# The next-to-last chunk's routing runs as one block ahead of the last units' masks, and its scatters run beside each other

## The chip, the cores and the metric

The kernel runs on one core of a Trainium2 chip. Times are microseconds on the device for one execution; of several executions the median is given. In the rows of the trace the engines are PE (TensorE, matrix products), PEld (its weight loads), DVE (VectorE), ACT (ScalarE), POOL (GpSimd) and SP (SyncE, which here only issues transfers; SPq and POOLq are the parts of SP and GpSimd that issue). L785 is line 785 of the kernel before.

## What is computed

The reference has two stages. The first is a linear attention with a complex decay, for 4 batches, 8 heads, 768 time steps and head size 48. The second is a mixture of experts on its output: 3072 tokens of 384 values, 8 experts, each token sent to at most one.

```python
for t in range(S):                       # first stage
    ar, ai = (a_re_n[:, :, t, :, None], a_im_n[:, :, t, :, None])
    new_re = ar * S_re - ai * S_im
    new_im = ar * S_im + ai * S_re
    kv = np.einsum('bhd,bhe->bhde', k[:, :, t], v[:, :, t])
    S_re, S_im = (new_re + kv, new_im)
    y[:, :, t] = np.einsum('bhd,bhde->bhe', q[:, :, t], S_re)
...
do_compute = x @ w_skip > 0              # second stage, x is y by token
e_idx = np.argmax(xc @ w_gate, axis=1)   # xc: the tokens with do_compute
...
h = np.maximum(xc[mask] @ w1[e], 0.0)    # mask: the tokens of expert e
y[mask] = gate_w[mask, None] * (h @ w2[e])
out[do_compute] = xc + y                 # the others pass unchanged
```

## The kernel before

**Attention.** The 768 steps are cut into 6 chunks of 128 steps (`c` from 0 to 5), and each chunk into 4 units, one for each batch (`b`). A unit forms its scores `pa` on TensorE (`unit_at`), masks them into `at` on VectorE (L657, two halves), and combines them with the state of the chunks before. For the last chunks (`late`) that is done with two products on VectorE, `RX` (L667 with the state, L668 with a copy of the state whose halves are swapped, `T2`, made by two transfers, L641), and their sum, `st` (L679). Then come the output `py` (L703 from `at`, L706 from `st`), its copy `yT`, and the product `px` (L713), which turns the rows into token order and at once gives the 9 routing numbers per token. The rows go to `xa`, and from there to the output (L727).

**Routing.** For chunks 0 to 4, `route` works on all four batches together. From the routing numbers `lg` it makes, on VectorE, the sum over heads `lgs` (L805), the best expert, and `oh`, which marks it; TensorE counts the tokens ahead of each one that go to the same expert (L827 to L830); VectorE then makes the row `sl` (L852) in a table `xs` in device memory, which holds 240 rows for each expert. `place` scatters each batch's 128 tokens to these rows with an indirect transfer that GpSimd issues (L785). The scheduler knows that all of them write `xs`, so each waits for the one before, except those of chunk 5, for which `place` declares that they don't touch the same rows. Chunk 5's routing is done for each unit by itself (`route1`, `rest`).

**Experts.** Expert 0's input is put together on TensorE without waiting for all scatters: chunk 5's tokens are picked by products with a one-hot matrix `ohx` (L1053), and those of chunks 0 to 4 are read from `xs` into the tile `early` (L744) and transposed into the same sums (L1050). Chunk 5's own scatters wait for that read. Experts 1 to 7 get their rows by `xg` (L1017) from `xs`. Weights come by SP into four buffers (L998), and ScalarE and VectorE split each one in two (L1009, L1010). The expert products are L1085 and L1117 to L1119.

**What sets the order.** The kernel is written as generators (`units`, `router`, `weights` and others), and `Order` decides, by a priority and by estimated times, which one writes its next instructions. A scheduler then lays the instructions out for each engine; `tc.issue_after(x)` keeps an instruction behind `x`. Each engine works through its own list in order, and so does SP. The tile tagged `T2` has one buffer: the next unit's copy can only be made when this unit's L668 has read it.

Of the kernel before, what the change touches and what calls it, by code (L numbers as in the profile page):

```python
# [24 lines left out]
NCH = S // C  # L25
# [14 lines left out]
BIG = float(1 << 20)  # L40


P_UNIT, P_ROUTE, P_CONSUME, P_REST, P_GATE, P_WEIGHTS = 0.5, 0.7, 1, 1, 2, 3

SHARE = 1.8
CREDIT = 600.0
# [66 lines left out]
class Kern:  # L113
# [530 lines left out]
    def unit(self, c, b):  # L644
# [8 lines left out]
        pa = self.pa.pop((c, b))  # L653
        for hh in range(2):

            with self.tc.issue_after(self.cins):
                self.at_ins = V.tensor_tensor(at[:, hh * 4:hh * 4 + 4], pa[hh],  # L657
                                              self.mask.rearrange("p (o t) -> p o t", o=1).to_broadcast([128, 4, C]),
                                              ALU.mult).ins
            yield o.wait(vt(512), 0 if hh == 0 or c == 0 else self.rx_t)  # L660
        late = self.last(c)
        Fb = self.F[:, :, b * H:(b + 1) * H].unsqueeze(3) if c > 0 else None
        if c > 0:
            T = self.T[b]
            X = self.un.tile([96, 2, H, D], F32, name=f"RX_{nm}", tag="RX", bufs=1)
            if late:
                V.tensor_tensor(X[:, 0], T, Fb[:, 0].to_broadcast([96, H, D]), ALU.mult)  # L667
                V.tensor_tensor(X[:, 1], self.T2.pop(b), Fb[:, 1].to_broadcast([96, H, D]), ALU.mult)  # L668
            else:
                with self.tc.issue_after(self.cins):  # L670
                    V.tensor_tensor(X, T.unsqueeze(1).to_broadcast([96, 2, H, D]), Fb.to_broadcast([96, 2, H, D]), ALU.mult)
# [42 lines left out]
        self.px_ins = pe.ins  # L714
        xa = self.xa[:, b]
        if c == NCH - 1:
            V.tensor_reduce(self.lg[:, b], px[:, :, 2 * D:].rearrange("p h e -> p e h"), AX.X, ALU.add)
        else:
            A.copy(self.lg[:, b], px[:, :, 2 * D:])
        if c == NCH - 1:  # L720
# [16 lines left out]
    def early(self):  # L737

        m = self.rt.tile([128, B * XW], F32, name="early", tag="xa", bufs=2)
        o = self.un.tile([128, B, CAP], F32R, name="ohx", tag="qkT")  # L740
        nx = 2 * DM
        self.xe = m[0:TP, 0:nx].rearrange("p (t d) -> p t d", d=DM)
        self.ohx = [o[:, b] for b in range(B)]
        self.early_ins = self.nc.sync.dma_start(self.xe, self.xs[0:CAP, 0:DM].rearrange("(t p) d -> p t d", p=TP)).ins  # L744

    def units(self, g):
        self.nat(2 * g, 0)
        self.nat(2 * g, 1)
        self.unit_at(2 * g, 0)
        for cc in range(2):  # L750
            c = 2 * g + cc
            while self.routes_done < c - 1:
                yield 0, 200
            if c > 0:
                yield from self.make_F(c - 1)
            if c < NCH - 1:
                self.lg = self.rt.tile([128, B, H // 2, E + 1], F32, name=f"lg_{c}", tag="lg", bufs=2)
            else:
                self.lg = self.rt.tile([128, B, E + 1], F32, name=f"lg_{c}", tag="lg5")
            self.xa = self.rt.tile([128, B, XW], F32, name=f"xa_{c}", tag="xa", bufs=2)  # L760
            if c == NCH - 1:
                self.parts = [self.un.tile([128, B, DM], F32R, name=f"xa{k}", tag="nat") for k in "hl"]
            self.nc.gpsimd.tensor_copy(self.xa[:, :, DM], self.tok[:, :, c])
            for b in range(B):

                while self.cpos < min((g + 1) * (HC + 1) + (cc * B + b) * PACE, NG * (HC + 1)):
                    yield 0, 100
                yield from self.unit(c, b)
                self.units_done += 1
            if c < NCH - 1:  # L770
                self.routes.append((self.lg_t, self.route(c, self.lg, self.xa)))

    def router(self):

# [9 lines left out]
    def place(self, c, b, sl, xa):  # L784
        x = self.nc.gpsimd.indirect_dma_start(out=self.xs, out_offset=bass.IndirectOffsetOnAxis(ap=sl, axis=0),  # L785
                                              in_=xa[:, b], in_offset=None, bounds_check=E * CAP - 1, oob_is_err=False).ins

        if c == NCH - 1:
            for y in self.scat:
                self.tc.declare_no_dep(x, y, reason="no two tokens have the same row")  # L790
            self.behind(x, [self.early_ins])
            self.scat.append(x)

    def route(self, c, lgp, xa):
# [27 lines left out]
        yield tiny, 130  # L822
        V.tensor_tensor(oh, self.iota8, b1(am), ALU.is_equal)
        yield sm, 130
        V.tensor_tensor(oh, oh, b1(act), ALU.mult)
        pr = self.ps_m.tile([128, B, E], F32, name=f"pr_{c}", tag="m")
        PE.matmul(pr, self.tri, oh, start=True, stop=False)  # L827
        PE.matmul(pr, self.ones, self.ohs.unsqueeze(1).to_broadcast([128, B, E]), start=False, stop=False)
# [20 lines left out]
        sl = self.rt.tile([128, B], I32, name=f"sl_{c}", tag="sl", bufs=4)  # L849
        V.tensor_tensor(rk, rk, base, ALU.add)  # L850
        yield tiny, 130
        V.tensor_tensor(sl, rk, ov, ALU.add)  # L852
        for b in range(B):
            self.place(c, b, sl[:, b:b + 1], xa)
        yield tiny, 0
# [9 lines left out]
    def route1(self, b):  # L865

        V, PE = self.nc.vector, self.nc.tensor
        c = NCH - 1
        T = lambda name, sh, dt=F32: self.rt.tile([128, B] + sh, dt, name=f"{name}_{c}", tag=name)
        iota = self.iota8[:, 0]  # L870
        sm, tiny = vt(8), vt(1)
        if b == 0:
            self.r5 = [T(k, []) for k in ("mx", "am", "act")] + [T("cand", [E]), T("oh", [E], BF16), T("dl", [E])]
            self.pr5 = self.ps_s.tile([128, B, E], F32, name="pr5", tag="ps")
        mx, am, act, cand, oh, dl = self.r5
        one = lambda t: t[:, b:b + 1]
        L, pr = self.lg[:, b, 0:E], self.pr5[:, b]
        V.tensor_reduce(one(mx), L, AX.X, ALU.max)
        yield sm, 70
        V.scalar_tensor_tensor(cand[:, b], L, one(mx), iota, ALU.is_equal, ALU.mult)  # L880
        yield sm, 70
        V.tensor_scalar(one(act), self.lg[:, b, E:], 0.0, None, ALU.is_gt)
        V.tensor_reduce(one(am), cand[:, b], AX.X, ALU.min)
        yield sm + tiny, 70
        V.scalar_tensor_tensor(oh[:, b], iota, one(am), one(act).to_broadcast([128, E]), ALU.is_equal, ALU.mult)
        PE.matmul(pr, self.tri, oh[:, b], start=True, stop=False)
        for k in range(b):
            PE.matmul(pr, self.ones, oh[:, k], start=False, stop=False)
        self.pr_ins[b] = PE.matmul(pr, self.ones, self.ohs, start=False, stop=True).ins
        pt = self.order.pe(200)  # L890
        hi, lo = [t[:, b] for t in self.parts]
        V.tensor_tensor(lo, self.xa[:, b, 0:DM], hi, ALU.subtract)
        yield self.order.wait(vt(DM), pt)
        if b == 0:
            self.early()

        val = T("val", [])[:, 0:1]
        V.scalar_tensor_tensor(val, oh[:, b, 0:1], -BIG, pr[:, 0:1], ALU.mult, ALU.add)
        yield tiny, 70
        V.tensor_scalar(self.ohx[b], self.iotac, BIG, val, ALU.subtract, ALU.is_equal)  # L900
        yield vt(CAP), 0
        if b >= B - 2:
            self.order.add(P_REST, self.rest(0 if b == B - 2 else b, b + 1))
# [436 lines left out]
```

## Time and profile before

| what | us |
|---|---|
| median of 3 runs | 531.55 |
| lowest and highest of them | 530.05, 532.46 |
| the profiled execution, its own time | 526.55 |
| its span in the trace | 524.8 |
| TensorE busy | 406.7 (77% of the span) |
| VectorE busy | 405.9 (77%) |
| ScalarE busy | 301.3 (57%) |
| GpSimd busy | 99.1 (19%) |

Shares of the whole span say little here, since the stages differ: in the first VectorE is the fullest engine, in the second (from about 380 us) TensorE. A wait between the two stages is in neither share. The granted clock is given as a part of TensorE's full speed.

### The profile page before, as it was taken

How to read it: one execution, taken by the hardware profiler on the slowest of the kernel's cores; microseconds unless marked ns; L12 is line 12 of the kernel's file. 1: busy time of each engine (PE TensorE's matmuls, PEld its weight loads, DVE VectorE, ACT ScalarE, POOL GpSimd, SP SyncE). 2: the span in 40 equal slices, each digit the busy share in tenths (PEclk: the TensorE clock that was granted, in tenths of full speed). 3: DMA queues.
4: the chain of work that ended last, by engine and by line, in shares of the span. 5: the costliest groups of instructions: out<-in, count | busy, mean ns of one | idle time of the engine just before them, and what ended most of it. 6: DMA issues, size and time to landing. Idle time of an engine off the chain costs nothing. (4 is left out here: it accounts for less than half of the span.)

```text
span 524.8 us, 9901 instructions
## 1 busy us (share of the span) xinstructions
PE 406.7 (77%) x3200; PEld 353.3 (67%) x3200; DVE 405.9 (77%) x1051; ACT 301.3 (57%) x685; POOL 99.1 (19%) x174
## 2 busy tenths in 40 slices
PE   0347534499899304999999999986399999999993
PEld 0125322379777202887888889976399999999993
DVE  3899988989999999989789747877079678666731
ACT  5778867655557754788868651333066547554620
POOL 4002011111122544000000321201311112111011
PEclk9966777579999656999999999999599999999998
DMA  5557876679989887777555358556268678666400
GB/s 95 114 109 176 187 177 140 140 180 218 226 194 228 209 201 188 192 169 169 135 141 134 81 137 276 151 141 214 71 185 275 217 248 253 180 212 229 118 22 25
DMA packets 165217, 88.63 MB, mean 169 GB/s; under 512 B 138939, under 2 KB 158860, under 8 KB 165159
## 3 DMA queue, kind: packets, MB, share of 16 engines
q1 hardware_dynamic: 158135, 72.09, 54.1%
q0 software_dynamic: 5936, 15.65, 10.6%
q8 instruction: 27, 0.44, 0.4%
q10 hardware_dynamic: 1088, 0.20, 0.2%
q14 instruction: 31, 0.25, 0.2%
HBM read 63.19 MB, written 26.58 MB: 171 GB/s over the span
## 5 line engine op out<-in xcount | busy, mean ns | idle before, releaser
L496 PE MATMUL sw<-ws,ident 128*128 128x384 f32 x84 | 44.9, 672 | 36.3 <-ACT ws L482 36.3
L413 DVE TENSOR_TENSOR X<-W,ain 128x192 f32<-128x192 f32 x192 | 67.8, 353 | 3.5 <-ACT ain L339 0.2
L1010 DVE TENSOR_TENSOR l<-r,h 128x768 fp32r<-128x768 f32 (+1 forms) x53 | 56.5, 1072 | 11.2 <-ACT h L1009 11.2
L1087 ACT ACTIVATE hh<-ph 128x240 fp32r<-128x240 f32 x64 | 23.8, 374 | 56.3 <-PE ph L1085 56.1
L496 PEld LDWEIGHTS sw<-ws,ident 128*128 128x128 f32 x84 | 19.4, 254 | 48.7 <-ACT ws L482 39.0
L1009 ACT CAST h<-r 128x768 fp32r<-128x768 f32 (+1 forms) x53 | 49.1, 934 | 4.9 <-DMA r<-in_moe_w_dram 4.6
L422 DVE TENSOR_TENSOR W<-X 128x96 f32<-128x96 f32 x192 | 48.8, 254 | 3.6
L1085 PE MATMUL ph<-xh,l 128*128 128x240 f32 x192 | 51.2, 274 | 0.0
L1085 PE MATMUL ph<-xh,h 128*128 128x240 f32 x192 | 49.6, 274 | 0.0
L1085 PE MATMUL ph<-xl,h 128*128 128x240 f32 x192 | 49.5, 276 | 0.0
L578 PE MATMUL tp<-ident,iw 128*96 128x128 f32 x128 | 22.8, 324 | 30.1 <-DVE iw L514 25.6
L585 ACT COPY qk<-tp 96x256 f32<-96x256 f32 x128 | 39.7, 369 | 7.8 <-PE tp L578 7.6
L1117 PE MATMUL po<-h,hh 128*120 128x384 f32 x128 | 43.2, 338 | 0.0
L1118 PE MATMUL po<-l,hh 128*120 128x384 f32 x128 | 42.9, 337 | 0.0
L657 DVE TENSOR_TENSOR at<-pa,mask 128x512 f32<-128x512 f32 x48 | 32.3, 684 | 11.1 <-PE pa L635 7.0
L1119 PE MATMUL po<-h,hl 128*120 128x384 f32 x128 | 40.9, 341 | 0.0
L785 POOL DMA_INDIRECT xs<-xa,sl x24 | 26.9, 1120 | 73.9 <-DVE sl L852 20.6
L703 PE MATMUL py<-at,vt 128*64 128x128 f32 x384 | 40.4, 282 | 0.0
L578 PEld LDWEIGHTS tp<-ident,iw 128*96 128x96 f32 x128 | 17.3, 151 | 34.1 <-issue 10.9
L635 PE MATMUL pa<-qk 96*128 96x128 f32 x256 | 35.9, 289 | 4.3 <-DVE at L657 4.0
L635 PEld LDWEIGHTS pa<-qk 96*128 96x128 f32 x256 | 32.0, 197 | 8.5 <-DVE at L657 5.3
L1088 DVE SCALAR_TENSOR_TENSOR hl<-ph,hh 128x240 fp32r<-128x240 f32 x64 | 25.7, 403 | 14.8 <-ACT hh L1087 14.7
(241 smaller groups left out, 1062.0 us busy)
## 6 DMA issues: line engine op xcount, KB each, us to landing
r<-in_moe_w_dram SPq DMA_DIRECT2D x24, 512.0 KB, 4.7
r<-in_moe_w_dram SPq DMA_DIRECT2D x32, 384.0 KB, 4.0
nat<-kq SPq DMA_DIRECT2D x8, 768.0 KB, 5.4
kq<-nw POOLq DMA_DIRECT2D x24, 192.0 KB, 3.7
kq<-iw POOLq DMA_DIRECT2D x24, 192.0 KB, 2.9
vt<-in_v_dram SPq DMA_DIRECT2D x24, 192.0 KB, 3.3
out_dram<-xa SPq DMA_DIRECT2D x24, 192.0 KB, 3.2
ain<-in_a_im_dram SPq DMA_DIRECT2D x90, 48.0 KB, 2.5
```

What stands on the lines that cost most here:

```text
L413: V.tensor_tensor(X, prev.unsqueeze(1).to_broadcast([128, 2, 2, D]), windows(ain[:, j]), ALU.mult)
L422: self.cins = V.tensor_tensor(W[:, j, ::-1], X[:, :, 0], X[:, :, 1], ALU.add).ins
L496: nc.tensor.matmul(sw, self.ident, ws[:, :, c], start=(c == 0), stop=(c == 1))
L578: nc.tensor.transpose(tp[:, jj], src[:, s * 4 + jj], self.ident)
L635: nc.tensor.matmul(pa[h // 4][:, h % 4], KT(h), QT(h), start=True, stop=True)
L703: PE.matmul(py[j * 64:j * 64 + 64, hp], vt_[:, 2 * hp + j], at[:, 2 * hp + j], start=True, stop=(c == 0))
L1009: nc.scalar.copy(hi[:, ks], raw)
L1010: nc.vector.tensor_tensor(lo[:, ks], raw, hi[:, ks], ALU.subtract)
L1085: pe = PE.matmul(ph, w[:, k, js], x[:, k], start=(n == 0), stop=(n == len(terms) - 1))
L1117: PE.matmul(po, hh[:, j, sl], w2h[:, j], start=(j == 0), stop=False)
L1118: PE.matmul(po, hh[:, j, sl], w2l[:, j], start=False, stop=False)
L1119: pe = PE.matmul(po, hl[:, j, sl], w2h[:, j], start=False, stop=(j == NF - 1))
```

## The change

Chunk 4's routing (`c == NCH - 2`) is no longer handed to the `router` but runs with a higher priority than the units (`P_SOON`), and the instructions of units 2 and 3 of chunk 5 on VectorE (masks and state products) are kept behind it (`pin`, `rins`). Its four scatters are declared not to touch the same rows, as chunk 5's were, and `early` waits for all four (`behind`). Unit 0 of chunk 5 copies its routing numbers with ScalarE, and VectorE sums them later, when the routing of chunk 4 is done.

```diff
-P_UNIT, P_ROUTE, P_CONSUME, P_REST, P_GATE, P_WEIGHTS = 0.5, 0.7, 1, 1, 2, 3
+P_SOON, P_UNIT, P_ROUTE, P_CONSUME, P_REST, P_GATE, P_WEIGHTS = 0.4, 0.5, 0.7, 1, 1, 2, 3
...
-            with self.tc.issue_after(self.cins):
+            pin = self.rins if c == NCH - 1 and b >= 2 else self.cins
+            with self.tc.issue_after(pin):
                 self.at_ins = V.tensor_tensor(at[:, hh * 4:hh * 4 + 4], pa[hh],
...
             if late:
-                V.tensor_tensor(X[:, 0], T, Fb[:, 0].to_broadcast([96, H, D]), ALU.mult)
-                V.tensor_tensor(X[:, 1], self.T2.pop(b), Fb[:, 1].to_broadcast([96, H, D]), ALU.mult)
+                with self.tc.issue_after(pin):
+                    V.tensor_tensor(X[:, 0], T, Fb[:, 0].to_broadcast([96, H, D]), ALU.mult)
+                    V.tensor_tensor(X[:, 1], self.T2.pop(b), Fb[:, 1].to_broadcast([96, H, D]), ALU.mult)
...
         if c == NCH - 1:
-            V.tensor_reduce(self.lg[:, b], px[:, :, 2 * D:].rearrange("p h e -> p e h"), AX.X, ALU.add)
+            lgp = px[:, :, 2 * D:]
+            if b == 0:
+                self.lg0 = self.rt.tile([128, H // 2, E + 1], F32, name=f"lg_{nm}", tag="lg0")
+                A.copy(self.lg0, lgp)
+            else:
+                V.tensor_reduce(self.lg[:, b], lgp.rearrange("p h e -> p e h"), AX.X, ALU.add)
...
         self.early_ins = self.nc.sync.dma_start(self.xe, self.xs[0:CAP, 0:DM].rearrange("(t p) d -> p t d", p=TP)).ins
+        self.behind(self.early_ins, self.scat)
...
-            if c < NCH - 1:
+            if c < NCH - 2:
                 self.routes.append((self.lg_t, self.route(c, self.lg, self.xa)))
+            elif c < NCH - 1:
+                self.order.add(P_SOON, self.soon(c, self.lg_t, self.route(c, self.lg, self.xa)))
+
+    def soon(self, c, t, r):
+        while self.routes_done < c:
+            yield 0, 100
+        yield self.order.wait(0, t)
+        yield from r
...
-        if c == NCH - 1:
+        if c >= NCH - 2:
             for y in self.scat:
                 self.tc.declare_no_dep(x, y, reason="no two tokens have the same row")
-            self.behind(x, [self.early_ins])
+            if c == NCH - 1:
+                self.behind(x, [self.early_ins])
             self.scat.append(x)
...
-        V.tensor_tensor(oh, oh, b1(act), ALU.mult)
+        ins = V.tensor_tensor(oh, oh, b1(act), ALU.mult).ins
+        if c == NCH - 2:
+            self.rins = ins
...
-        V.tensor_tensor(sl, rk, ov, ALU.add)
+        ins = V.tensor_tensor(sl, rk, ov, ALU.add).ins
+        if c == NCH - 2:
+            self.rins = ins
...
+        while self.routes_done < c:
+            yield 0, 100
         if b == 0:
+            V.tensor_reduce(self.lg[:, 0], self.lg0.rearrange("p h e -> p e h"), AX.X, ALU.add)
             self.r5 = [T(k, []) for k in ("mx", "am", "act")] + [T("cand", [E]), T("oh", [E], BF16), T("dl", [E])]
```

What this does to the engines' lists is seen at three places. Names end in the number of a buffer; `RX_5_2` is unit 2 of chunk 5, and `lgs_4` belongs to chunk 4.

VectorE before, from the first instruction of chunk 4's routing: its small instructions alternate with the masks and state products of units 2 and 3.

```order
L805 TENSOR_REDUCE lgs_4_4138<-lg_4_3811 128x36
L667 TENSOR_TENSOR RX_5_2_4254<-T_4_2_3974,F_4_4068 96x384
L810 TENSOR_REDUCE mx_4_4140<-lgs_4_4138 128x4
L821 TENSOR_SCALAR act_4_4142<-lgs_4_4138 128x4
L668 TENSOR_TENSOR RX_5_2_4254<-T2_5_2_4186,F_4_4068 96x384
L812 TENSOR_TENSOR cand_4_4147<-lgs_4_4138,mx_4_4140 128x32
L814 TENSOR_TENSOR dl_4_4148<-lgs_4_4138,mx_4_4140 128x32
L657 TENSOR_TENSOR at_5_2_4218<-pa_5_2_0_4176,mask_71 128x512
L817 TENSOR_TENSOR cand_4_4147<-cand_4_4147,iota8_94 128x32
L679 SCALAR_TENSOR_TENSOR st0_165<-RX_5_2_4254,sg_86 96x8x48
L834 TENSOR_REDUCE se_4_4143<-dl_4_4148 128x4
L819 TENSOR_REDUCE am_4_4141<-cand_4_4147 128x4
```

VectorE now, from the same instruction, and then the end of the routing:

```order
L822 TENSOR_REDUCE lgs_4_4139<-lg_4_3811 128x36
L827 TENSOR_REDUCE mx_4_4141<-lgs_4_4139 128x4
L838 TENSOR_SCALAR act_4_4143<-lgs_4_4139 128x4
L829 TENSOR_TENSOR cand_4_4148<-lgs_4_4139,mx_4_4141 128x32
L831 TENSOR_TENSOR dl_4_4149<-lgs_4_4139,mx_4_4141 128x32
L834 TENSOR_TENSOR cand_4_4148<-cand_4_4148,iota8_94 128x32
L836 TENSOR_REDUCE am_4_4142<-cand_4_4148 128x4
L853 TENSOR_REDUCE se_4_4144<-dl_4_4149 128x4
```

```order
L864 TENSOR_REDUCE rk_4_4147<-cand_4_4148 128x4
L866 TENSOR_SCALAR ov_4_4146<-rk_4_4147 128x4
L869 TENSOR_TENSOR rk_4_4147<-rk_4_4147,base_4_4145 128x4
L877 SCALAR_TENSOR_TENSOR todo_113<-ov_4_4146,act_4_4143 128x4
L871 TENSOR_TENSOR sl_4_4223<-rk_4_4147,ov_4_4146 128x4
L658 TENSOR_TENSOR at_5_2_4219<-pa_5_2_0_4177,mask_71 128x512
L658 TENSOR_TENSOR at_5_2_4219<-pa_5_2_1_4178,mask_71 128x512
L896 TENSOR_REDUCE lg_5_4083<-lg_5_0_4133 128x9
```

The 22 instructions of the routing, from `lgs` to `sl`, now stand in one piece; before, 18 instructions of units 0 to 3 stood among them. The two masks of unit 2 now come behind `sl`.

TensorE before, from the second half of unit 2's scores (`pa_5_2_1`): the counting matmuls `pr_4` came 12 rows later, within unit 3's scores.

```order
L635 MATMUL pa_5_2_1_4177<-qk_2_1_2168 128x128 x4
L635 MATMUL pa_5_3_0_4258<-qk_2_1_2168 128x128 x4
L713 MATMUL px_5_0_4128<-wg_100,yT_5_0_4126 128x105 x4
L703 MATMUL py_5_1_4190<-at_5_1_4137,vt1_164 64x128 x2
L706 MATMUL py_5_1_4190<-qk_2_1_2168,st1_166 64x128 x2
```

TensorE now:

```order
L635 MATMUL pa_5_2_1_4178<-qk_2_1_2168 128x128 x4
L846 LDWEIGHTS tri_75
L846 MATMUL pr_4_4160<-oh_4_4150,tri_75 128x32
L847 LDWEIGHTS ones_78
L847 MATMUL pr_4_4160<-ohs_111,ones_78 128x32
L849 LDWEIGHTS ones_78
L849 MATMUL pr_4_4160<-oh_4_4150,ones_78 128x24
L849 LDWEIGHTS ones_78
L849 MATMUL pr_4_4160<-oh_4_4150,ones_78 128x16
L849 LDWEIGHTS ones_78
L849 MATMUL pr_4_4160<-oh_4_4150,ones_78 128x8
L715 MATMUL px_5_0_4128<-wg_100,yT_5_0_4126 128x105 x4
```

The five counting matmuls moved ahead of unit 0's `px` and unit 1's `py`.

SP before, from the copies of the swapped state for unit 3 (`T2_5_3`) to `early`:

```order
L641 DMA T2_5_3_4268<-T_4_3_4039 48x384 x2
L727 DMA out_0_dram<-xa_5_4084 128x384
L632 DMA vt1_164<-in_v_dram 128x8x48
L727 DMA out_0_dram<-xa_5_4084 128x384 x2
L998 DMA r3_1_0_4562<-in_moe_w1_dram 128x1024
L998 DMA r3_1_1_4566<-in_moe_w1_dram 128x1024
L998 DMA r3_1_2_4570<-in_moe_w1_dram 128x1024
L998 DMA r8_1_0_4576<-in_moe_w2_dram 128x2x384
L727 DMA out_0_dram<-xa_5_4084 128x384
L744 DMA early_4339<-xs_117 120x2x384
```

SP now, from the first output write of chunk 5:

```order
L734 DMA out_0_dram<-xa_5_4084 128x384
L632 DMA vt1_164<-in_v_dram 128x8x48
L641 DMA T2_5_3_4274<-T_4_3_4039 48x384 x2
L751 DMA early_4307<-xs_117 120x2x384
L734 DMA out_0_dram<-xa_5_4084 128x384 x2
L1022 DMA r3_1_0_4564<-in_moe_w1_dram 128x1024
L1022 DMA r3_1_1_4568<-in_moe_w1_dram 128x1024
L1022 DMA r3_1_2_4572<-in_moe_w1_dram 128x1024
L1022 DMA r8_1_0_4578<-in_moe_w2_dram 128x2x384
```

The two copies of `T2_5_3` moved behind an output write and a load of `v`, and `early` moved from the end of this piece to directly behind these copies: it now stands ahead of two output writes and of the first four weight loads of expert 1 (`r3_1_0` to `r8_1_0`).

## Rows read from the trace of the kernel before

**Rows 1.** The page's slices of the whole span, 13.1 us each.

```profile
PE   0347534499899304999999999986399999999993
```

**Rows 2.** Chain that ended last, 353 to 384: start, us, what.

```profile
367.00 0.97 DMA xs<-xa,sl
370.09 2.42 DMA xs<-xa,sl
372.72 3.50 DMA early<-xs
```

**Rows 3.** Timeline of POOL: start, us, engine, line, operation, out<-in, idle before.

```profile
356.83 1.00 POOL L785 DMA_INDIRECT xs<-xa,sl  x1 [18.47 <-DVE xal L892]
359.92 0.97 POOL L785 DMA_INDIRECT xs<-xa,sl  x1 [2.08 <-ACT dl L916]
377.01 0.97 POOL L785 DMA_INDIRECT xs<-xa,sl  x1 [5.95 <-DMA early<-xs]
380.85 0.97 POOL L785 DMA_INDIRECT xs<-xa,sl  x1 [0.30 <-ACT xh L1056]
```

**Rows 4.** Timeline of VectorE (DVE), columns as in rows 3.

```profile
344.94 0.39 DVE L805 TENSOR_REDUCE lgs<-lg 128x36 f32<-128x144 f32 x1
351.01 0.55 DVE L668 TENSOR_TENSOR RX<-T,F 96x384 f32<-96x384 f32 x1 [0.73 <-DMA T<-T]
353.74 0.60 DVE L679 SCALAR_TENSOR_TENSOR st<-RX,sg 96x384 f32<-96x384 f32 x1
355.88 0.15 DVE L852 TENSOR_TENSOR sl<-rk,ov 128x4 int32<-128x4 f32 x1
361.63 0.17 DVE L922 TENSOR_SCALAR ov<-rk 128x3 f32<-128x3 f32 x1
361.83 0.16 DVE L926 TENSOR_TENSOR rk<-rk,base 128x3 f32<-128x3 f32 x1
```

**Rows 5.** Timeline of TensorE (PE), columns as in rows 3.

```profile
345.71 1.16 PE L635 MATMUL pa<-qk 96*128 96x128 f32 x8
358.48 0.39 PE L706 MATMUL py<-qk,st 96*64 96x128 f32 x4
363.62 0.17 PE L889 MATMUL pr<-ohs,ones 128*128 128x8 bf16 x1
376.27 2.92 PE L1050 MATMUL pt<-ident,early 120*128 120x120 f32 x12 [12.48 <-DMA early<-xs]
380.20 0.27 PE L1085 MATMUL ph<-xh,h 128*128 128x240 f32 x1
```

**Rows 6.** Busy us by stretch: PE, PEld, DVE, ACT, POOL, clock, DMA, GB/s.

```profile
345.71:363.79 18.08, 16.08 (x191) 14.77 (x189) 14.80 (x81) 6.04 (x15) 1.98 (x2) 1.00 0.54 151
364.00:376.00 12.00, 0.00 (x0) 0.00 (x0) 0.99 (x9) 0.00 (x0) 1.94 (x2) 0.60 0.47 162
376.00:380.20 4.20, 3.93 (x18) 3.93 (x19) 0.12 (x1) 0.36 (x1) 2.58 (x3) 0.51 0.12 44
380.20:400.00 19.80, 19.80 (x151) 19.63 (x150) 16.77 (x38) 12.60 (x23) 2.70 (x5) 1.00 0.73 216
165.00:205.00 40.00, 13.57 (x85) 8.92 (x84) 38.35 (x130) 23.35 (x52) 21.12 (x28) 0.63 0.81 193
```

**Rows 7.** Timeline of SP's DMA issues, columns as in rows 3.

```profile
347.37 1.15 SPq L641 DMA_DIRECT2D T<-T  x2
359.83 1.88 SPq L998 DMA_DIRECT2D r<-in_moe_w_dram  x4
384.57 1.32 SPq L1017 DMA_DIRECT2D xg<-xs  x3
```

**Rows 8.** Timeline of ScalarE (ACT), columns as in rows 3.

```profile
385.54 3.69 ACT L1009 CAST h<-r 128x1024 fp32r<-128x1024 f32 x4
```

**Rows 9.** All 24 scatters: ns min/median/max, first and last start.

```profile
L785 POOL DMA_INDIRECT xs<-xa,sl x24: 967/1024/2762, 167.9 to 380.8; - x24
```

## The prediction

> **What bounds the kernel now.** I first read the slices of the whole span [rows 1]. TensorE is nearly full from the 17th slice to the end except for one hole around the 29th. A hole in an engine that is otherwise full is time that can be given back, so the chain that ended last is the next view: back from the last output write it is TensorE all the way, until it leaves TensorE for transfers, two scatters into `xs` and then the read `early` [rows 2]. TensorE's own rows put the price on it: the transposes of `early` (L1050) start at 376.27 after 12.48 us idle, and what TensorE did before was the last small routing matmul, 363.62 + 0.17 = 363.79 [rows 5]. [...] So this place is bound by a wait for one transfer, plus a slow restart, and everything after it by TensorE.
>
> What is late is then followed back. `early` may leave only when chunk 4's four scatters have landed; they start at 356.83, 359.92, 367.00 and 370.09, each one after the one before has landed [rows 2, 3]. One alone costs 370.09 - 367.00 = 3.09 us from start to start; the second cost 7.08 us, with four weight loads issued at 359.83 beside it [rows 3, 7]. Last, the first scatter waits for `sl` at 355.88, though the routing that makes it began with `lgs` at 344.94 [rows 4].
>
> **The routing in one block.** It still begins at 344.94: the rows ahead of it keep their order. A chain of dependent small VectorE instructions runs at 0.20 us a step (361.63 to 361.83) [rows 4]. From `lgs` (0.39 us) to `oh` times `act` are six steps: 344.94 + 0.42 + 1.2 = 346.56. The counting matmuls are now right behind `pa_5_2_1`, which starts at 345.71 and takes 1.16: 346.87 [rows 5]. Five of them at no more than 0.17 each: 347.0 to 347.7. Five more steps to `sl`: 348.0 to 348.7, against 355.88. I take 348.4, since the small matmuls overlap in part. If all 22 instructions were in line one behind the other, 22 x 0.20 + 0.85 gives 350.2, the upper bound.
>
> **The scatters.** The first starts 0.8 us after `sl` is written (355.88 + 0.15 to 356.83), so at 349.35. Without the wait they follow each other like the last chunk's four, which have none: (380.85 - 377.01) / 3 = 1.28 us [rows 3]. The last starts at 353.2. From a start to the landing are 2.63 us (370.09 to 372.72) [rows 2]; with the weight loads it was 7.08, but those now stand behind `early` on SP's queue. So `early` leaves at 355.8, and takes 3.55 us (372.72 to 376.27): landed at 359.4, between 359.0 and 361.2 by the bounds of `sl`. TensorE wants it after its last routing matmul, 363.79 before the change. The wait is gone, with some 4 us to spare.
>
> **What is late next** is the end of the routing of unit 3 on TensorE. Between 345.71 and 363.79, 18.08 us, TensorE is busy 16.08 [rows 6], so this stretch can shrink by 2.0 at the very most. What can lengthen it: unit 2's masks wait for the block (to about 348.6), and so does its second state product, which frees the buffer of the swapped state of unit 3. That copy is issued at 347.37 now and used at 351.01, 3.64 us [rows 4, 7]; behind the block and the two masks and products (four instructions, about 0.6 each) it leaves at about 351.0 and is there at 354.6. Unit 3's `st` follows at about 356.1 (353.74 before), and TensorE asks for it at 358.48 [rows 4, 5], so up to 2.3 us more stay covered by TensorE's own work; the cost is nothing, and past that it counts fully. I take -0.5 us, with -2.0 and +1.0 as ends.
>
> **The restart.** From the first L1050 to the first expert matmul were 380.20 - 376.27 = 3.93 us for 18 matmuls at half clock [rows 5, 6]. After no idle time they run at the full one: 2.0 us, and 2.1 with the copy of `xh` that the first expert matmul waits for. So the first expert matmul comes at 363.79 - 0.5 + 2.1 = 365.4 instead of 380.20: **14.8 us** earlier.
>
> **Whether the experts can use it.** Expert 1's first four loads (three of 512 KB, one of 384 KB by the shapes in the code) leave at 359.83 and are first used at 385.54, 5.34 after the first expert matmul [rows 7, 8]; now that is 370.7. They still wait for the copy of unit 2's rows, so leave at about 359.5; at the 216 GB/s of the stretch after the hole [rows 6] 1.97 MB need 9.1 us: 368.6. That covers them with 2 us, where it was 17. The gathers `xg` leave when chunk 5's scatters have landed, 384.57, 4.4 us after the first expert matmul [rows 7]. Those scatters now wait for their own `sl`, not for `early`: the last starts at about 366.3, lands at 369, 3.6 after the first expert matmul. They keep their place. Extra work is one copy and one reduce moved behind it, beside TensorE: nothing.
>
> **Sum.** The profiled execution took 526.55 us: 526.55 - 14.8 = 511.8. The three runs have a median of 531.55, 5.0 above it. I take the same 14.8 off the median: **516.8 us**, 2.8% faster. Less than 0.5% (2.7 us) can hardly be told from no change.
>
> **Rivals.** (a) *The scatters stay slow*, since descriptors are now written on GpSimd while VectorE is busy, where two of the four found it idle. Scatters range from 0.97 to 2.76 us [rows 9], eight of them lie in a stretch where VectorE is busy 38.35 of 40 us [rows 6]. At 2.76 + 0.31 each the last starts at 358.6 and ends at 361.3, landing 1.66 later (2.63 - 0.97), 363.0; `early` is there at 366.5, and TensorE waits 3.2 us: 520.0. Against it stands the median of 1.02. [...]
> (b) *The scatters still go one by one*: 349.35 + 3 x 3.09 + 2.63 = 361.2, `early` there at 364.8, a wait of 1.5 us: 518.3. The moved routing alone is nearly enough, so this would hardly show in the time.
> (c) *Expert 1's weights come late*: they share the engines with chunk 5's scatters and with `early`. Every us past 370.7 delays ScalarE's casts and, soon, TensorE: 1 to 5 us, 518 to 522.
> (d) *No change*: the experts are bound by their loads, so that an earlier start is waited away. Against it: TensorE is busy 19.80 of 19.80 us behind the hole [rows 6], and nothing but TensorE is on the chain behind it. 531.
> (e) *Slower*: SP works in order, and `early` now stands in front of two writes and four loads, and behind the copies for unit 3, which wait for VectorE's block. If that chain holds `early` beyond 372.72, all that stands behind it is late too; from there each us costs one. At 3 us: 534. It would need 17 us more than worked out above.
>
> **Numbers.** Forecast 0.68, with a range of its own from 515 to 518.5; (a) 0.09, (b) 0.04, (c) 0.12, (d) 0.04, (e) 0.03. The 5 us between the profiled execution and the median leave the size open, so the range of 8 in 10 goes from 512.5 to 522.5; it takes in (a), (b) and most of (c). Faster by over 0.5%: all but (d) and (e), 0.93; within 0.5% 0.04; slower 0.03.
>
> **What would show it.** `sl` of chunk 4 within 5 us of its `lgs`; four scatters 1.3 us apart from about 349; `early` issued by 357; L1050 following the last routing matmul without idle time and at a clock of 1.00; first expert matmul near 365. An idle row at L1050 that names `early` speaks for (a) or (b); idle time of ScalarE's casts for the loads of expert 1 and of TensorE behind them for (c). The prediction is wrong if TensorE's routing ends past 365, or if a new hole opens behind the first expert matmul.

## The result, and the profile after

| | us | of the kernel before |
|---|---|---|
| kernel before, 4 executions | median 531.97 (530.05 to 532.46) | |
| changed kernel, 4 executions | median 517.06 (515.98 to 524.85) | 0.9719, 95% interval 0.9682 to 0.9757 |
| profiled execution, before | 526.55, span 524.8 | |
| profiled execution, after | 516.39, span 514.7 | |

Executions that took over 1.5% longer than the fastest of the same kernel (524.85 us here, 525.24 and 522.21 us in after_fourth) are left out of every ratio, though not out of the medians. The change is faster, and 516.8 was forecast. But the medians differ by 14.9 us and the two profiled executions by 526.55 - 516.39 = 10.2 us: the forecast took its 14.8 us from the trace, and in the trace they are not all there. So the size needs looking at.

VectorE's rows of the changed kernel (start, duration, then engine, line, operation, output and inputs), at the place of [rows 4]:

```profile
345.52 0.39 DVE L822 TENSOR_REDUCE lgs<-lg 128x36 f32<-128x144 f32 x1
...
348.56 0.16 DVE L871 TENSOR_TENSOR sl<-rk,ov 128x4 int32<-128x4 f32 x1
...
356.37 0.55 DVE L670 TENSOR_TENSOR RX<-T,F 96x384 f32<-96x384 f32 x1
357.03 0.61 DVE L681 SCALAR_TENSOR_TENSOR st<-RX,sg 96x384 f32<-96x384 f32 x1
```

GpSimd's rows, as [rows 3]:

```profile
349.52 0.98 POOL L801 DMA_INDIRECT xs<-xa,sl  x1 [12.56 <-DVE at L658]
350.80 1.02 POOL L801 DMA_INDIRECT xs<-xa,sl  x1 [0.30 <-issue]
352.13 0.97 POOL L801 DMA_INDIRECT xs<-xa,sl  x1 [0.30 <-issue]
353.40 0.98 POOL L801 DMA_INDIRECT xs<-xa,sl  x1 [0.30 <-issue]
363.81 0.97 POOL L801 DMA_INDIRECT xs<-xa,sl  x1 [9.43 <-DVE oh L909]
...
367.64 0.97 POOL L801 DMA_INDIRECT xs<-xa,sl  x1 [0.30 <-issue]
```

SP's issues, as [rows 7]:

```profile
356.05 0.43 SPq L751 DMA_DIRECT2D early<-xs  x1
...
360.34 1.89 SPq L1022 DMA_DIRECT2D r<-in_moe_w_dram  x4
...
370.39 2.08 SPq L1041 DMA_DIRECT2D xg<-xs  x3
```

The first half went as worked out. From `lgs` to `sl` are 3.04 us instead of 10.94; chunk 4's scatters are 1.27 to 1.33 us apart; `early` is issued at 356.05, where 355.8 was forecast and 372.72 stood before. The chain of what ended last, at the place of [rows 2] and [rows 5]:

```profile
364.30 1.44 PE pt L1074 x12
365.74 0.68 PE pt L1077 x6
366.41 2.18 issue
368.60 4.80 PE ph L1109 x27
```

Busy time by stretch, as [rows 6] (stretch, length, PE, PEld, DVE, ACT, POOL with their counts, granted clock, DMA share, GB/s):

```profile
364.00:366.00 2.00, 2.00 (x23) 1.98 (x22) 1.61 (x13) 0.00 (x0) 1.70 (x2) 1.00 0.89 322
366.00:368.00 2.00, 0.41 (x4) 0.22 (x2) 0.00 (x0) 0.00 (x0) 1.39 (x3) 1.00 1.01 348
368.00:370.00 2.00, 1.40 (x6) 1.44 (x7) 1.12 (x4) 0.72 (x2) 0.61 (x1) 0.60 0.52 195
370.00:372.00 2.00, 2.00 (x12) 2.00 (x12) 0.36 (x1) 0.00 (x0) 0.00 (x0) 0.55 0.29 51
```

The wait of 12.48 us is gone and the transposes run at a granted clock of 1.00, 1.44 us. But a new hole of 2.18 us stands behind the last token matmuls, for which the trace names nothing ("issue"), and after it the granted clock is 0.60 and 0.55, near the 0.51 of the restart in [rows 6]. ScalarE and VectorE stand too. They wait to copy tiles whose last matmuls are recorded in the six of 365.74, and are released at 368.1 by something that the trace can't place ("remote"):

```profile
368.14 0.36 ACT L1078 CAST xh<-pt 128x240 fp32r<-128x240 f32 x1 [4.25 <-remote]
...
368.18 0.41 DVE L1079 CAST xh<-pt 128x240 fp32r<-128x240 f32 x1 [2.54 <-remote]
```

TensorE's first expert matmul reads what ScalarE copies here and starts 0.10 us behind the copy (368.14 + 0.36 = 368.50, then 368.60). So TensorE's hole follows from the late copy, and what is late is the release of ScalarE and VectorE.

### The profile page after: what moved, and what is told of

Same layout as the page of the kernel before. It is cut to its first block, busy times and chain, and to the rows that moved or that the text cites. A ratio compares the mean times of both kernels' runs of the same rounds, so it can differ in the third digit from the quotient of the medians.

```text
span 514.7 us, 9900 instructions
## 1 busy us (share of the span) xinstructions
PE 411.3 (80%) x3200; PEld 355.7 (69%) x3200; DVE 406.6 (79%) x1051; ACT 301.5 (59%) x686; POOL 97.0 (19%) x174
## 4 chain that ended last, share of the span: by engine, by line
PE 60%; DVE 12%; SPq 10%; DMA 8%; ACT 4%; issue 4%; POOL 0%; DVEq 0%; POOLq 0%; ACTq 0%
PE ph L1109 13%; SPq L232 10%; PE pa L635 6%; PE ps L694 5%; PE py L705 5%; PE po L1141 4%; PE po L1143 4%; PE po L1142 4%; PE px L715 3%; PE py L708 3%; PE tu L563 3%; PE tp L578 2%; PE sw L496 2%; DVE X L413 2%; DMA ain<-in_a_re_dram 2%
## 5 line engine op out<-in xcount | busy, mean ns | idle before, releaser
L1109 PE MATMUL ph<-xh,h 128*128 128x240 f32 x192 | 50.9, 279 | 2.2 <-issue 2.2
L1109 PE MATMUL ph<-xh,l 128*128 128x240 f32 x192 | 52.3, 279 | 0.0
L578 PE MATMUL tp<-ident,iw 128*96 128x128 f32 x128 | 24.4, 340 | 29.2 <-DVE iw L514 25.1
L1109 PEld LDWEIGHTS ph<-xh,h 128*128 128x128 f32 x192 | 36.5, 193 | 2.3 <-issue 2.3
L1109 PEld LDWEIGHTS ph<-xh,l 128*128 128x128 f32 x192 | 37.2, 194 | 0.0
```

The costliest lines, as they stand in the source:

```text
L578: nc.tensor.transpose(tp[:, jj], src[:, s * 4 + jj], self.ident)
L1109: pe = PE.matmul(ph, w[:, k, js], x[:, k], start=(n == 0), stop=(n == len(terms) - 1))
```

## The experiments

Beside every group of kernels the kernel before was timed on the same chip; each ratio is to that. In the table, all from the traces: where TensorE begins the transposes of `early`, where the first expert matmul starts, and how long it is from there to the end of the span. The names are those used below.

| trace | transposes | first expert matmul | between | from there to the end | ratio in time (95%) |
|---|---|---|---|---|---|
| before | 376.27 | 380.20 | 3.93 | 144.6 | |
| before_again | 374.97 | 378.96 | 3.99 | 145.4 | |
| after | 364.16 | 368.60 | 4.44 | 146.1 | 0.9719 (0.9682 to 0.9757) |
| after_again | 364.37 | 366.68 | 2.31 | 145.7 | 0.9786 (0.9743 to 0.9828) |
| after_third | 363.47 | 367.90 | 4.43 | 148.2 | 0.9816 (0.9777 to 0.9856) |
| after_fourth | 363.59 | 368.00 | 4.41 | 146.7 | 0.9753 (0.9717 to 0.9788) |
| free_only | 372.09 | 376.08 | 3.99 | 145.1 | 0.9895 (0.9863 to 0.9927) |
| ahead_only | 370.71 | 374.70 | 3.99 | 145.6 | 0.9855 (0.9816 to 0.9895) |
| no_hold | 369.05 | 373.05 | 4.00 | 145.4 | 0.9910 (0.9879 to 0.9941) |
| late_loads | 363.45 | 367.89 | 4.44 | 151.0 | 0.9915 (0.9882 to 0.9948) |
| more_bufs | 366.21 | 370.68 | 4.47 | 147.5 | 0.9822 (0.9780 to 0.9864) |
| late_scat | 367.55 | 369.86 | 2.31 | 150.5 | 0.9804 (0.9761 to 0.9847) |
| early_first | 363.78 | 368.04 | 4.26 | 144.9 | 0.9774 (0.9736 to 0.9812) |
| late_scat_bufs | 361.67 | 363.97 | 2.30 | 147.3 | 0.9755 (0.9707 to 0.9804) |

The stages ahead shift a whole trace by up to 4 us from one execution to the next (chunk 4's first scatter starts at 348.93 in after_fourth and at 352.88 in late_scat), so the two columns of differences tell more than the places. In early_first 18 other matmuls stand between the two, so its "between" is not to be compared with the others'.

**The same kernel again** (after_again), no edit.

> The changed kernel once more, unaltered. Two things are open after its first trace: TensorE, ScalarE and VectorE all stand from 366.4 to 368.1 us, between the last token matmul (L1077) and the first expert matmul (L1109, 368.60), and the 27 expert matmuls behind it take 4.80 us at half clock. Theory H1 (the stall belongs to the kernel: it comes from what runs on the queues just then): there is a gap of 1.5 to 3 us in this trace too, the first expert matmul is at 368 to 369, and the median is 516 to 518 us, a gain of 14 to 16 us over the kernel before. Theory H2 (a chance of that one execution): no gap over 0.5 us, first expert matmul at 366.3 to 366.8, full clock from there, and a span that is 3 to 4 us shorter, 511 us.

Median 515.01 against 526.69. In this trace there is no hole. The chain first, then rows of ScalarE and TensorE from expert 1 on:

```profile
364.51 1.44 PE pt L1074 x12
365.95 0.68 PE pt L1077 x6
366.62 0.05 issue
366.68 2.15 PE ph L1109 x17
```

```profile
380.10 0.83 ACT L1033 CAST h<-r 128x768 fp32r<-128x768 f32 x1 [3.81 <-DMA r<-in_moe_w_dram]
...
383.31 0.44 PE L1141 MATMUL po<-h,hh 128*120 128x384 f32 x1 [0.35 <-ACT hh L1111]
385.23 0.38 PE L1109 MATMUL ph<-xl,h 128*128 128x240 f32 x1 [0.16 <-DVE xl L1063]
```

The hole was absent here and back in the third and fourth trace, so neither H1 nor H2 holds as it stands: it comes and goes between executions of one program. Without it, 2.1 us of restart is nearly right (2.31), and ScalarE's copy comes as TensorE's last token matmuls end (366.22 + 0.36 = 366.58, the first expert matmul at 366.68). Then the next thing is late: ScalarE waits 3.81 us for expert 1's fifth load, what it owes TensorE queues behind that, and TensorE idles twice, 0.51 us in all. From expert 1's first transposes (379.73) to the end are 132.7 us, 1.05 more than the 131.6 of before (393.18 to 524.8). The second trace of before has 132.0 for the same stretch, so the loss is 0.5 to 1 us: rival (c), at or under its lowest price of 1 us.

**The kernel before again** (before_again), no edit.

> The kernel before once more, unaltered, for a second trace of it: its profiled execution took 526.55 us, its other executions 530.05 to 532.46. Theory B1 (the 5 us lie in TensorE's wait for the early rows): in an execution of some 531 us the wait in front of L1050 is 16 to 18 us instead of 12.48, and the change, which removes that wait, gains 15 us. Theory B2 (the 5 us lie elsewhere, in the stages ahead of 346 us or behind 380 us): the wait in front of L1050 is 11.5 to 13.5 us again, the experts' stage starts later by what an earlier stage lost, and then the mechanism of the prediction pays some 10 us, as the two first traces show, and the other 5 us of the median's gain come from something that the two programs share.

526.17 us, TensorE's wait 12.20. An execution of some 531 us was wanted, and this one is as short as the first, so the 4 to 5 us between before's profiled execution and its first medians are not placed by it. But the medians of before in the four later comparisons, on four chips, are 526.69, 527.33, 528.57 and 528.72, none near 531.97, while the changed kernel has 515.0 to 517.8 everywhere. B1 could not be tested on an execution of 531 us; it stays open.

**Free scatters alone** (free_only): before, plus this.

```diff
+        self.behind(self.early_ins, self.scat)
...
-        if c == NCH - 1:
+        if c >= NCH - 2:
             for y in self.scat:
                 self.tc.declare_no_dep(x, y, reason="no two tokens have the same row")
-            self.behind(x, [self.early_ins])
+            if c == NCH - 1:
+                self.behind(x, [self.early_ins])
```

> Only half of the change: chunk 4's scatters wait for each other no more, its routing stays in the old place. By the rows of before: first scatter at 356.8, four of them 1.28 us apart, the last at 360.7, the load of the early rows leaves 2.6 us later, at 363.4, behind expert 1's first four loads on SP, and lands 3.6 us later at 367.0 if it shares nothing with them, at 371 if it waits for all their data. TensorE restarts at half clock, 3.9 us, first expert matmul at 371 to 375 against 380.2: a gain of 5 to 9 us, 523 to 527 us. Rival (the scatters are kept apart by the transfers and not by the waits): they stay 3 us and more apart, and the time stays over 529 us.

Median 522.01 against 526.69. Rows of GpSimd, SP and TensorE in order of time:

```profile
358.53 1.00 POOL L786 DMA_INDIRECT xs<-xa,sl  x1 [18.03 <-DVE xal L894]
359.83 0.98 POOL L786 DMA_INDIRECT xs<-xa,sl  x1 [0.30 <-issue]
...
361.70 0.93 SPq L1000 DMA_DIRECT2D r<-in_moe_w_dram  x2
...
362.39 0.98 POOL L786 DMA_INDIRECT xs<-xa,sl  x1 [0.31 <-issue]
...
368.14 0.41 SPq L744 DMA_DIRECT2D early<-xs  x1
...
372.09 2.91 PE L1052 MATMUL pt<-ident,early 120*128 120x120 f32 x12 [6.44 <-DMA early<-xs]
```

The rival falls: it was the declared wait that kept them apart, 1.28 to 1.30 us without it. The last scatter, with weight loads issued just ahead of it, needs 368.14 - 362.39 = 5.75 us to release `early`, where 2.63 stood for an undisturbed one, so a wait of 6.44 us and the slow restart, 3.99 us, remain. The first expert matmul, at 376.08, is later than the 371 to 375 that were expected, and the gain in the medians, 4.7 us, is a little under the expected 5 to 9.

**Routing ahead alone** (ahead_only): the change, with the old condition in `place`.

> The other half: the routing runs ahead as in the change, the scatters wait for each other as before. They start at 349.5, 352.6, 355.7 and 358.8 (3.1 us apart, as the first two of before), the early rows leave at 361.4 and land at 365.0, against 364.16 at which TensorE asks for them in the changed kernel: 0.9 us more, 517 to 519 us. Rival (SP): chunk 5's stores and expert 1's loads stand behind the early load on SP and leave 5.4 us later (365.7 instead of 360.3); if expert 1 waits for them, 520 to 523 us.

Median 518.85 against 526.69. Rows of GpSimd and TensorE:

```profile
352.83 0.98 POOL L801 DMA_INDIRECT xs<-xa,sl  x1 [10.62 <-DVE at L658]
356.17 1.30 POOL L801 DMA_INDIRECT xs<-xa,sl  x1 [2.36 <-issue]
361.11 0.97 POOL L801 DMA_INDIRECT xs<-xa,sl  x1 [3.64 <-issue]
364.20 0.97 POOL L801 DMA_INDIRECT xs<-xa,sl  x1 [2.12 <-issue]
...
370.71 2.91 PE L1073 MATMUL pt<-ident,early 120*128 120x120 f32 x12 [4.69 <-DMA early<-xs]
```

One by one, the four take 3.3, 4.9 and 3.1 us from start to start, and TensorE still waits 4.69 us. The median lies in the expected 517 to 519, but by luck: a wait of 0.9 us was expected, and the whole change, from which that was counted, has a median of 515.01 here, 3.8 us less. This wait also costs the slow restart, 3.99 instead of 2.31 us, at a granted clock of 0.50 from 370 to 374. So both halves are needed for the whole gain.

**Without the hold** (no_hold).

```diff
-            pin = self.rins if c == NCH - 1 and b >= 2 else self.cins
+            pin = self.cins
```

> The change without its hold: the masks and state products of the last two units are no longer held behind the last routing instruction, the rest is as in the change. By VectorE's order the routing then stands between the state products again, nearly as in the kernel before, and the load of the early rows stands behind two of expert 1's loads on SP. Theory (the hold is what moves the routing, the earlier turn in the plan does nothing by itself): the first scatter at 356 to 359, as with the free scatters alone, TensorE waits 5 to 7 us for the early rows, and the time is that of the free scatters alone, 0.985 to 0.993 of the kernel before. Rival (the earlier turn is enough): first scatter before 352, no wait, the time of the whole change.

Rows of GpSimd and TensorE:

```profile
355.75 1.00 POOL L801 DMA_INDIRECT xs<-xa,sl  x1 [19.57 <-DVE xal L916]
...
369.05 2.92 PE L1074 MATMUL pt<-ident,early 120*128 120x120 f32 x12 [2.81 <-DMA early<-xs]
```

The first scatter is as late as in before, TensorE waits 2.81 us, and the ratio (0.9910) can't be told from that of the free scatters alone (0.9895). A wait of 5 to 7 us was expected, so that size was wrong; but where the routing stands, the theory is borne out: it is the hold behind `rins` that brings it forward (first scatter at 348.77 in the next trace, with the hold), not its earlier turn in the plan.

**The same kernel a third time** (after_third), base of no_hold and of the next two.

> The changed kernel unaltered, as the base that the next three are compared with, and a third trace of it. Its first trace had a hole of 2.18 us in front of the first expert matmul (368.60), its second had none (366.68, 2.3 us after the transposes of the early rows began). Theory H2 (the hole is a chance of single executions): most likely no hole again, first expert matmul 2.1 to 2.5 us after the transposes begin, the median 11 to 12 us under the kernel before. Theory H1 (it belongs to the kernel and the second trace was the exception): a hole of 1.5 to 3 us.

517.75 against 527.33. The hole is back at 2.18 us, against what was held more likely. TensorE's row:

```profile
367.90 0.43 PE L1109 MATMUL ph<-xh,h 128*128 128x240 f32 x1 [2.18 <-issue]
```

**Expert 1's loads later** (late_loads).

```diff
                 self.raw_ins = nc.sync.dma_start(raw, src[:, ks]).ins
+                if e == 1 and not k and n == KD:
+                    self.behind(self.raw_ins, [self.ph0_ins])
...
                     self.ph_ins = pe.ins
+                    if e == 0 and j == 0:
+                        self.ph0_ins = pe.ins
```

> The change, and expert 1's loads on SP also wait for TensorE's first group of expert matmuls, so that they leave some 7 us later, at 367.7 instead of 360.6. Theory W (with the wait for the early rows gone, expert 1's weights stand on the path, with 1 us lost on them already in the second trace): the first four land at 373 to 374 instead of before 372, ScalarE and VectorE get them 1 to 2 us late, the later loads follow, TensorE waits 1.5 to 3 us more between 379 and 390, and the time is 1.5 to 3 us over the change. Rival (there is slack in these loads, and by leaving they take their traffic off the stores and scatters in front of the experts): the same time as the change or up to 1 us less, first expert matmul at the same place.

Median 522.14, 4.4 us over the change's. The loads left at 370.60, 10.9 us later than in after_third, not 7. Rows by stretch, columns as above:

```profile
366.00:368.00 2.00, 0.11 (x1) 0.14 (x2) 0.53 (x2) 0.36 (x1) 1.60 (x2) 1.00 0.24 88
368.00:370.00 2.00, 1.73 (x14) 1.53 (x15) 0.95 (x3) 0.36 (x1) 0.00 (x0) 1.00 0.14 49
...
386.00:390.00 4.00, 2.50 (x20) 2.31 (x21) 3.36 (x13) 3.24 (x6) 0.00 (x0) 1.00 0.79 285
390.00:394.00 4.00, 2.49 (x20) 2.10 (x19) 4.00 (x9) 2.57 (x5) 1.03 (x1) 1.00 0.83 260
```

Two things follow. The direction of theory W is shown, its size was too small: TensorE stands 3.0 of the 8 us from 386 to 394, and a delay of 10.9 us costs 4.4, so 10.9 - 4.4 = 6.5 us of delay were covered, with the hole in the trace. By the traces it is less: from expert 1's transposes to the end are 137.4 us here and 131.5 in after_third, 5.9 more, and part of that doesn't show in the time because the granted clock behind this hole was 1.00 (from 368 to 382), where after_third has 0.50 from 368 to 374. And the hole is there again, 2.18 us, while the transfers take 0.24 of the DMA engines instead of 1.01: these loads don't make it. (Nor does a fetch of instructions in the first trace: of the 505 packets that lie in its hole, from 366.41 to 368.60, 380 are of queue q1 and 125 of q0, none of an instruction queue.)

**One staging buffer more** (more_bufs).

```diff
-                                   for n, b in (("mr2", 4), ("m1", 1), ("mx", 2), ("mh", 2))]
+                                   for n, b in (("mr2", 5), ("m1", 1), ("mx", 2), ("mh", 2))]
...
-                            if n == 3:
+                            if n == 4:
```

> The change with five staging buffers instead of four for the raw weights, and expert 1's fifth load ahead of the three token loads on SP: it leaves at 362.5 instead of 374.8. Theory W (expert 1's weights are on the path): ScalarE finds the fifth load there and no longer waits 3.8 us for it, the second halves come 1 us earlier, TensorE's idle time of 0.5 us between 382 and 386 goes, first expert matmul unchanged, and the span from it to the end shrinks by 0.5 to 1.2 us. That is 0.1 to 0.2 per cent, at the edge of what the times can tell; the trace decides. Rival (the weights aren't on the path): ScalarE's wait goes, the span from the first expert matmul to the end stays within 0.3 us.

Median 517.80, the time of the change (517.75). This trace has the hole, and in it expert 1's weights reach TensorE in time anyway: from expert 1's transposes to the end are 131.54 us here and in after_third. So it does not test what happens without the hole.

**The same kernel a fourth time** (after_fourth), base of the next two.

> The changed kernel unaltered, as the base for the two beside it on the same chip, and a fourth trace. The hole of 2.18 us in front of the first expert matmul was there in the first and third trace and absent in the second; it was also there, 2.18 us long, with expert 1's loads moved out of its way, so those loads don't make it. Expected: the hole again with two chances in three (first expert matmul 4.4 us after the transposes begin, span of 514 to 516), otherwise 2.3 us after, span of 512.

516.71 against 528.57, hole of 2.15 us.

**Chunk 5's scatters later** (late_scat).

```diff
-            self.place(c, b, sl[:, b - b0:b - b0 + 1], self.xa)
+            self.held.append((b, sl[:, b - b0:b - b0 + 1]))
...
         hi = A.copy(xh[:, 2], pts[2]).ins
+        for b, sl in self.held:
+            self.place(NCH - 1, b, sl, self.xa)
+            self.behind(self.scat[-1], [hi])
```

> The change, and chunk 5's four scatters on GpSimd wait until ScalarE has copied the last of expert 0's token tiles, so that GpSimd issues nothing while TensorE runs the transposes and the last token matmuls. Theory S (the hole comes from these scatters: in the traces with a hole they start 0.35 us before the transposes, and TensorE goes on just as the last of the four ends on GpSimd): no hole, the first expert matmul 2.2 to 2.5 us after the transposes begin, at full clock; the scatters start at 366.6 instead of 363.8, expert 1's tokens are fetched 2.5 us later, at 374, which the 13 us up to their transposes hide; 512 to 515 us. Rival (the scatters have nothing to do with it): the same hole of 2.18 us, and the time of the change or 0 to 1 us more.

TensorE's rows:

```profile
367.55 1.58 PE L1074 MATMUL pt<-ident,early 120*128 120x120 f32 x12
...
369.86 0.35 PE L1112 MATMUL ph<-xh,h 128*128 128x240 f32 x1
```

No hole: 2.31 us from the one to the other. But the time is not better, 517.82 against 516.71, where 512 to 515 was expected. The token loads leave at 377.83, 8.0 us after the first expert matmul instead of 3.4, expert 1's remaining weights stand behind them, and TensorE waits 2.0 us for ScalarE; from there to the end are 150.5 us.

**Transposes earlier** (early_first).

```diff
-        for i, (b, x) in enumerate(((0, self.py_ins[2]), (1, px), (2, px), (-1, pr[3]), (3, pr[3]))):
+        for i, (b, x) in enumerate(((0, self.py_ins[2]), (1, px), (-1, px), (2, px), (3, pr[3]))):
```

> The change, with the transposes of the early rows on TensorE 18 matmuls earlier: ahead of unit 2's token matmuls and unit 3's routing. They begin some 1 us earlier, before the last scatters. Theory T (the hole belongs to the transposes, wherever they stand): token matmuls and routing behind them come 2.2 us late, the first expert matmul is still 3.5 to 4.5 us behind the transposes and its 18 matmuls. Theory S (chunk 5's scatters): the hole stays where the scatters run, behind the last token matmuls, or goes if the transposes must meet them. No hole at all in this order would leave 0.6 us for the last unit's routing, which nothing covers any more: 513 to 515 us.

TensorE's rows:

```profile
367.08 0.35 PE L1077 MATMUL pt<-ohx,xah 128*128 128x240 f32 x1 [1.00 <-issue]
...
368.04 0.35 PE L1109 MATMUL ph<-xh,h 128*128 128x240 f32 x1
```

One idle stretch of 1.00 us behind the last routing matmuls, where 0.6 was worked out for the routing alone, and a granted clock of 1.00 from there to 390. Nothing stalls right behind the transposes, which speaks against theory T. One trace can't refute it, since the changed kernel itself has one trace without the hole. The time can't be told from the change's (0.9774 and 0.9753).

**Late scatters and one buffer more** (late_scat_bufs): the edits of more_bufs, and late_scat with the scatters behind TensorE's last token matmul.

> Two edits on the change together: chunk 5's scatters wait for TensorE's last token matmul (in the first trial for ScalarE's last copy, 1 us later), and five staging buffers with expert 1's fifth load ahead of the token loads, so that the token loads, which the late scatters delay, hold back no weights of the first five. Theory S (these scatters make the hole): no hole a second time, the first expert matmul 2.2 to 2.5 us after the transposes begin, full clock. Theory W for the rest (in the first trial TensorE then waited 2.0 us and more between 382 and 390 for expert 1's weights and ScalarE behind them): it now waits under 1 us there, the span from the first expert matmul to the end is 145 to 146 us, and the time is 1 to 2.5 us under the change's, a ratio of 0.970 to 0.977 to the kernel before. Rival (the hole is chance, no matter what GpSimd does): a hole of 2.18 us, ratio 0.976 to 0.985.

515.17 against 528.72. Again no hole, 2.30 us. The expectation for the rest failed: ScalarE waits 5.53 us for a load and TensorE behind it 1.63, and to the end are 147.3 us instead of 145 to 146. TensorE's row:

```profile
381.00 0.44 PE L1144 MATMUL po<-h,hh 128*120 128x384 f32 x1 [1.63 <-ACT hh L1114]
```

The first expert matmul is the earliest of all traces (363.97), and what that gains is largely waited away. The ratio, 0.9755, lies inside three of the four intervals of the changed kernel run as it is, and its own interval overlaps the fourth: no version here can be told to beat the change.

## Why the prediction was right, and where it was off

**The bound and the mechanism: right.** TensorE's wait for `early` was the loss. The wait is 12.48 and 12.20 us in the traces of before, 6.44, 4.69 and 2.81 with parts of the change, none with all of it, and the first expert matmul moves with it.

**The routing in one block and the scatters: right.** 348.4 was forecast for `sl`, 348.56 came (the block began 0.58 us later than forecast and took 0.42 less); 355.8 for `early`, 356.05 came. Rival (a) is out: in after_again the first three of the four lie in a stretch where VectorE is busy 3.97 of 4.00 us:

```profile
350.00:354.00 4.00, 4.00 (x52) 3.73 (x51) 3.97 (x14) 1.54 (x4) 2.05 (x3) 1.00 0.83 238
```

and they take 0.98, 1.03, 0.97 and 0.98 us. The median of 1.02 that the prediction sets against rival (a) is that of all 24 scatters; the eight under the busy VectorE have 1.06.

**What is late next: right but for the sign.** The copy for unit 3 left at 352.07 instead of 351.0 and its `st` came at 357.03 instead of 356.1, still covered. TensorE reached the transposes at 364.16, not 363.29: +0.4 to before instead of -0.5, 0.9 us less gain. Unit 2's scores, where the forecast stretch begins, started 0.37 us later than in before (346.08, not 345.71), and from there it is the 18.08 us of before: the stretch did not shrink, and nothing new made it longer.

**The restart: the step that was mis-sized.** 2.1 us were forecast from the transposes to the first expert matmul; 2.31 came in one trace of the changed kernel, 4.41 to 4.44 in three, because of a hole that nothing in the trace of before shows. In the first trace it cost 2.3 us, and the lower clock behind it (0.60 and 0.55) about 1.6 more: 14.58 us to expert 1's transposes (383.18) instead of 12.98. That second cost varies: after_third, with the same hole, takes 16.66 us for this stretch, 3.7 more than before, with a granted clock of 0.50 from 368 to 374. The first expert matmul came at 368.60, not near the 365 that was named as a sign.

**Whether the experts can use it: a load left out of the sum.** 2 us of cover were forecast for expert 1's first four loads, and these were in time: in after_again ScalarE casts them at 372.07 without waiting. Late is the fifth. It needs one of the four buffers back, so it can't leave before VectorE has read the first load (374.78; with five buffers, in more_bufs, it leaves with the first four). The forecast has no term for it, though ScalarE waited for it in before too, where TensorE lost nothing by it. A row of before and one of after_again:

```profile
392.55 0.83 ACT L1009 CAST h<-r 128x768 fp32r<-128x768 f32 x1 [2.79 <-DMA r<-in_moe_w_dram]
...
372.07 3.69 ACT L1033 CAST h<-r 128x1024 fp32r<-128x1024 f32 x4
```

In the trace with no hole 0.5 to 1 us is lost to it; in late_scat_bufs, where later loads are late, more.

**The sum.** In the traces 14.8 becomes 14.8 - 0.9 - 2.3 - 1.5 = 10.1 us (524.8 - 514.7); in after_again 14.8 - 1.1 - 0.2 - 1.1 = 12.4 (524.8 - 512.4). The ratios of the four comparisons are worth 14.9, 11.3, 9.7 and 13.1 us. So that the first met the number 516.8 is luck in part: its median of before lies 3 to 5 us over those of the later comparisons, which no trace explains. The later comparisons put the change at 10 to 13 us, 1.8 to 2.5%.

**The other rivals.** (b) was priced far too low: it said that the moved routing alone would be nearly enough, with a wait of 1.5 us. The trace has 4.69, since one of the steps takes 4.9 us instead of 3.1, and the restart is at half clock again (0.50). Why that step is long isn't shown: the DMA engines are busy 0.55 of the time from 354 to 358 and 0.23 from 358 to 362. (d) and (e) did not come.

## What to carry to other kernels

A hole removed from a full engine is worth at most the distance to the next thing that is late; work out that distance for each stream that the work behind the hole consumes, here the next expert's weights, since it shrinks by all that is gained. A wait of TensorE cost twice here, by its length and by the slow restart (3.93 to 4.00 us behind waits of 2.81 to 12.48 us, 2.31 without one), so a remedy that left a short wait still paid the restart: with 2.81 us of wait left (no_hold) 4.0 of the 9.6 us in the medians were gained, with 4.69 us (ahead_only) 7.8 of 11.7. And a gain worked out from one trace is best checked trace against trace, for the difference of two medians can hold something else.

## What was not expected of the hardware

The hole: 2.15 to 2.22 us long in five of the six traces in which chunk 5's scatters begin on GpSimd 0.35 us ahead of the transposes (after, after_third, after_fourth, late_loads, more_bufs), TensorE, ScalarE and VectorE all standing (ScalarE up to its copy, 0.46 us ahead of TensorE's first expert matmul in each of the five), TensorE going on as the last scatter ends on GpSimd (367.64 + 0.97 = 368.61 and 368.60 in the first trace). It was absent from both traces in which those scatters were held back, and where the transposes stood earlier TensorE idled 1.00 us, 0.6 of it by the estimate for the routing alone. That points to the scatters. It doesn't settle it: after_again has them at the same place and no hole, so two traces without one could be chance, and in before, before_again, free_only, ahead_only and no_hold the four scatters start 0.7 us behind the start of the transposes, run beside them, and no hole follows. The cause stays open.

The clock after the hole: 0.60 and 0.55 in the first trace, 0.50 from 368 to 374 in after_third, but 1.00 in late_loads, behind a hole of the same 2.18 us.
